# Two attention and gated-MLP layers, one token, float32 cache: larger loads at the ends of passes, one more unit kept on chip, another order of loads

## The chip, the core and the metric

The kernel runs on one core of one Trainium2 chip. The metric is device time in microseconds of one execution, the median of several. The engines are TensorE (PE, with its weight loads as PEld), VectorE (DVE), ScalarE (ACT), GpSimd (POOL) and SyncE (SP); the last one only issues DMAs here. "L364" is line 364 of the kernel before.

## The reference

Two rows x of 448 numbers go twice through an attention block over a cache and a gated MLP. Each (batch, head) pair has 4096 keys and values of 256 numbers, so the caches are 2 x 16 x 4 MiB each and are read in both passes.

```python
B, Sq, D = 2, 1, 448
H, Sk, Dh = 16, 4096, 256          # F = 1792
def _A_ref(x, k_cache, v_cache, wq, wo):
    q = (x @ wq).reshape(B, Sq, H, Dh) ...
    scores = jnp.einsum("bhqd,bhkd->bhqk", q, k_cache) * (Dh ** -0.5)
    p = _softmax(scores, axis=-1)
    o = jnp.einsum("bhqk,bhkd->bhqd", p, v_cache)
    return ... @ wo
def _B_ref(x, W_gate, W_up, W_down):
    gate = gate * (gate > 0);  h = gate * up
    return jnp.einsum("bsf,fd->bsd", h, W_down)
x = x + _A_ref(_layernorm(x), ...)
x = x + _B_ref(_layernorm(x), ...)
x = x + _A_ref(_layernorm(x), ...)
x = x + _B_ref(_layernorm(x), ...)
```

## The kernel before

**Storage.** One SBUF tile, `arena`, has 27 slots ("units") of 128 x 2048 float32, 1 MiB each: six blocks of four slots (0 to 23) and three singles (24 to 26). The keys of one (head, batch) are four units, and so are its values; a head's weights (wq and wo columns) are one unit of 896 KiB; the MLP weights are seven units "in" and four units "out". A "whole" load fills one block with one DMA of 128 x 8192; the other loads fill one slot with 128 x 2048 or 128 x 1792.

**Loads.** `pending` is one list of all loads in the order of issue, and `pump` (L111) issues from its front as long as a place is free: one free slot for a single load, four free slots of one block for a whole one. It is called whenever the program releases a slot. All these DMAs are issued by SP, in order, each waiting on SP until the last reader of its slot is done. They rotate over eight semaphores, so an issue also waits until the load eight places before it has landed. `grouped` (L157) makes whole loads of keys and values except near the ends of a list: `ENDS = 12` keys from the end of a pass are single, and so are the first `SMALL = 25` of pass two.

**Passes.** Pass one runs the 32 steps (0,0), (0,1) ... (15,1), pass two runs them backwards, so its first steps find keys and values that pass one left on chip: `keep` has the 20 first units of pass two, one more unit (the last quarter of the values of step (14,1), `("v", second[2], NC - 1)`) and the weights of head 15. They are not loaded again. That leaves five other slots (two of a block that holds values of (14,1), three singles; the fifth is slot 2) for the MLP weights between the passes. All other keys, values and weights are read again.

**A step u** (`attention`, L280; loop at L502). DVE multiplies keys with the query and reduces (whole and not kept: `score_block`, L355, two multiplications over 16 tiles at L364 and one reduction at L373, while ACT sums eight tiles at L369; unit by unit otherwise: `score`, L378, for a kept unit eight fused instructions at L405, for others L396, L402 and ACT's L398). Then `softmax_max` (L414, L416), `softmax_exp` on ACT (L421, L424), `weigh` on PE (L443: four matmuls per unit), and one step later `out_copy` (ACT, L456), `out_add` (DVE, L459), `out_turn` (PE, L467), `out_keep` (DVE, L476) and `project` (PE, L486). Each engine works in program order. `busy(n)` (L226) is a matmul that nobody reads, put between the last step's quarters of `weigh`.

**The MLP** (`ffn`, L535). `proj` (L545) takes 16 matmuls for the gate (L551; parts 0, 1, 2, 3) and 16 for the up part (3, 4, 5, 6) and releases each "in" unit when it is used up; part 3 holds the last rows of both and is used twice. Then hid is multiplied (L613), transposed (L618, L620), and `block` (L634) computes each of four groups of output columns by 14 matmuls (L641). An ACT copy (L669 in the last layer, L710 in the first) takes each group from PSUM to SBUF. Before, all groups lie side by side in one PSUM region `pd`. In the first layer the four "out" loads, the first keys and two heads' weights of pass two follow the "in" loads in the same queue.

Of the kernel before, what the change touches and what calls it, by code (L numbers as in the profile page):

```python
# [8 lines left out]
F32 = mybir.dt.float32  # L9
AF = mybir.ActivationFunctionType  # L10
# [4 lines left out]
B, D, H, S, DH, F = 2, 448, 16, 4096, 256, 1792  # L15
P = 128
DC = 5
FULL, TAIL = 3, 64
# [3 lines left out]
NC = NT // CT  # L22
# [2 lines left out]

SUMS = 96
SMALL = 25
ENDS = 12
HASTE = 5
CLOSE = 4  # L30
BY_ACT = 3
# [35 lines left out]
def two_layers(  # L67
# [10 lines left out]
    nc = tc.nc  # L78
# [8 lines left out]
    ps_f = ctx.enter_context(tc.tile_pool(name="ps_f", bufs=2, space=PSUM))  # L87
# [7 lines left out]
    pending = []  # L95
# [35 lines left out]
    def get(*key):  # L131
        at = at_of[key]
        return arena[:, at * UNIT : (at + 1) * UNIT]
# [6 lines left out]
    second = first[::-1]  # L140

    def loads(order):
        found = [("h", order[0][0], 0)]
        for u, unit in enumerate(order):
            found.append(("k", unit, 0))
            if u > 0:
                found.append(("v", order[u - 1], 0))
            if u % 2 and u + 1 < len(order):
                found.append(("h", order[u + 1][0], 0))
        return found + [("v", order[-1], 0)]  # L150

    def cut(found):

        for kind, name, c in found:
            yield from ((kind, name, c + k) for k in range(NC if kind in "kv" else 1))

    def grouped(keys, begin, end):  # L157

        keys = list(keys)
        found, i = [], 0  # L160
        while i < len(keys):
            kind, name, c = keys[i]
            whole = kind in "kv" and c == 0 and begin <= i and i + NC <= len(keys) - end
            found.append((keys[i], NC if whole else 1))
            i += found[-1][1]
        return found

    ffn_loads = [("in", "", c) for c in range(7)] + [("out", "", c) for c in range(4)]
    of_first, of_second = list(cut(loads(first))), list(cut(loads(second)))

    keep = {of_second[0], *[key for key in of_second if key[0] != "h"][:KEPT]}
    keep.add(("v", second[2], NC - 1))
    of_second = [key for key in of_second if key not in keep]

    heads = [key for key in of_second if key[0] == "h"][:2]
    of_second = [key for key in of_second if key not in heads]
    of_second[NC - 1 : NC - 1] = heads
    pending += grouped(of_first, 0, ENDS) + [(key, 1) for key in ffn_loads]
    pending += grouped(of_second, SMALL, ENDS) + [(key, 1) for key in ffn_loads]

    row = consts.tile([P, 2 * DH], F32, name="row")
    down = consts.tile([P, D], F32, name="down")
# [35 lines left out]
    po_all = ps_o.tile([P, 2, 2 * DH], F32, name="po")  # L218
# [7 lines left out]
    def busy(n):  # L226


        unread = ps_q.tile([P, n * P], F32, name="pq")
        nc.tensor.matmul(  # L230
            unread[:B], ident[:, :B], ident[:, None, :].to_broadcast([P, n, P]),
            start=True, stop=True,
        )
# [46 lines left out]
    def attention(order, after, q_first=None, begun=None):  # L280
# [6 lines left out]
        n_u = len(order)  # L287
# [147 lines left out]
        def weigh(u, c):  # L435


            vt = get("v", order[u], c)
            if c == 0:
                po_of[u] = po_all[:, u % 2]  # L440
            for t in range(CT // 2):
                n = c * CT + 2 * t
                nc.tensor.matmul(  # L443
                    po_of[u][32 * t : 32 * t + 2, :],
                    p_of[u][:, n : n + 2],
                    vt[:, 2 * t * DH : (2 * t + 2) * DH],
                    start=(c == 0),
                    stop=(c == NC - 1),
                )
            if ("v", order[u], c) not in after:  # L450
                release("v", order[u], c)
            if u == n_u - 1 and c > 0:
                busy(4)

        def out_copy(u):
            nc.scalar.activation(row[:, :DH], po_of[u][:, :DH], AF.Copy, scale=lead[:, 0:1])  # L456
# [78 lines left out]
    def ffn(last):  # L535
# [9 lines left out]
        def proj(parts):  # L545

            p = ps_f.tile([P, D], F32, name="pf")
            for n, (part, c, done) in enumerate(parts):
                w = get("in", "", part)
                for j in range(4):  # L550
                    nc.tensor.matmul(  # L551
                        p[32 * j : 32 * j + 32, :],
                        xs[:, c, :32],
                        w[:, j * D : (j + 1) * D],
                        start=(n == 0),
                        stop=(n == 3),
                    )
                if done:
                    release("in", "", part)
                if part in (4, 5):  # L560
                    between(part)
            return p
# [24 lines left out]

        pg = proj([(0, 0, True), (1, 1, True), (2, 2, True), (3, 3, False)])  # L590
        add_rows(SUMS, lead, stop=last)
        if last:
            y_left = y[:, : FULL * P]
# [37 lines left out]
        stat = [hT[:, m, 32 * j : 32 * j + 32] for j in range(4) for m in range(FULL)]  # L631
        stat += [tails[:, m, :] for m in range(2)]

        def block(pd, c, chunks):  # L634

            width = P if c < FULL else TAIL
            at = slice(c * P, c * P + width)
            w = get("out", "", c)
            for k in chunks:
                g4 = k % 4  # L640
                nc.tensor.matmul(  # L641
                    pd[32 * g4 : 32 * g4 + 32, at], stat[k], w[:, k * width : (k + 1) * width],
                    start=(k < 4), stop=(k >= chunks[-1] - 3),
                )
            return at

        if last:


            square = work.tile([P, B], F32, name="square")  # L650
            nc.vector.tensor_mul(square, rstd, rstd)
            close = work.tile([P, CLOSE, B], F32, name="close")
            for i, st in enumerate(stat[-CLOSE:]):
                nc.vector.tensor_mul(
                    close[:, i, :], square, st.rearrange("p (b r) -> p b r", b=B)[:, :, 0]
                )
            unit = ident[SUMS : SUMS + B, SUMS : SUMS + B]
            y_end = ps_f.tile([P, TAIL], F32, name="pf")[SUMS : SUMS + B]
            nc.tensor.matmul(y_end, unit, y_end_row, start=True, stop=False)
            nc.tensor.matmul(y_left, unit, left, start=True, stop=False)  # L660
            pd = ps_f.tile([P, D], F32, name="pf")

            def to_y(at, stop):
                nc.tensor.matmul(y[:, at], scaled, down[:, at], start=False, stop=stop)

            for c in range(FULL):
                at = block(pd, c, range(14))
                release("out", "", c)
                nc.scalar.activation(down[:, at], pd[:, at], AF.Copy)  # L669
                if c > 0:  # L670
                    to_y(before, False)
                before = at
            at = block(pd, FULL, range(14 - CLOSE))
            nc.scalar.activation(down[:, at], pd[:, at], AF.Copy)
            to_y(before, True)
            nc.vector.tensor_copy(left, y_left)
            nc.sync.dma_start(found[:, : FULL * P], left)
            w = get("out", "", FULL)
            for i in range(CLOSE):
                k = 14 - CLOSE + i  # L680
                w_k = w[:, k * TAIL : (k + 1) * TAIL]
                nc.tensor.matmul(y_end, close[:, i, :], w_k, start=False, stop=False)
            nc.tensor.matmul(y_end, scaled, down[:, at], start=False, stop=True)
            nc.vector.tensor_copy(y_end_row, y_end)
            nc.scalar.dma_start(found[:, FULL * P :], y_end_row)
            return
# [14 lines left out]
                    start=False, stop=(c == FULL + 1),  # L701
                )

        pd = po_all[:, 0, :D]
        sums = work.tile([P, FULL + 1], F32, name="sums4")
        total = work.tile([P, 1], F32, name="sums")
        for c in range(FULL + 1):
            at = block(pd, c, range(14))
            release("out", "", c)
            nc.scalar.activation(down[:, at], pd[:, at], AF.Copy, accum_out=sums[:, c : c + 1])  # L710
            if c > 0:
                ask(c - 1)
            if c == FULL:
                nc.vector.reduce_sum(total, sums, axis=AX.X)
            pt = ps_s.tile([P, B], F32, name="small")
            found_in = [(spans[0][0], c)] if c < FULL else [(p, i.start) for p, i in spans[1:]]
            for p, _ in found_in:
                nc.tensor.matmul(pt[p], down[:, at], scaled, start=True, stop=True)
            for p, i in found_in:
                x_c = xr[p, i]  # L720
                nc.vector.tensor_add(x_c, x_c, pt[p, :, None].to_broadcast(x_c.shape))
# [85 lines left out]
```

## Time and profile before

| | |
|---|---|
| median of 3 runs | 1327.37 us (1326.68 to 1330.33) |
| profiled execution | 1327.61 us, span 1325.7 us |
| busy | PE 581.5, PEld 195.1, DVE 1004.0, ACT 325.1, POOL 106.2 us |
| SP's DMA queue | 562.58 MB, busy 99.5% of 16 engines' span |
| HBM read over the span | 562.56 MB, 424 GB/s |

The span is that of the profiled execution; the 1.9 us between it and its time lie outside of the instructions. In the rows of the timeline the columns are start, duration, engine, line, operation, tiles and count; what stands in brackets is the idle time of the engine just before and what ended it. Pass one ends near 668 us, the first MLP lies between 670 and 693 us, pass two ends near 1303 us and the second MLP runs to the end.

### The profile page before, as it was taken

Reading aid. Unit: us, or ns where it says so; the run is one execution under the profiler, and the core shown is the slowest. Engines: PE = TensorE matmul, PEld = TensorE weight load, DVE = VectorE, ACT = ScalarE, POOL = GpSimd, SP = SyncE. Lnnn points to the kernel's source line nnn. Section 1 sums busy time; section 2 is a strip of 40 time slices with the busy share of each in tenths; the row PEclk is TensorE's granted clock in tenths of the full one; section 3 lists DMA queues with packets and bytes.
Section 4 is the critical chain, followed back from the end, with each engine's and each line's share of the span. In section 5 each row is a group of like instructions: output and inputs, shape, how many; then the busy total and the mean of one; then the engine's idle time right before and its main releaser. Section 6 shows DMA issues by size and latency. Waiting matters only on the chain.

```text
span 1325.7 us, 9957 instructions
## 1 busy us (share of the span) xinstructions
PE 581.5 (44%) x3260; PEld 195.1 (15%) x3260; DVE 1004.0 (76%) x892; ACT 325.1 (25%) x1392; POOL 106.2 (8%) x192
## 2 busy tenths in 40 slices
PE   2434434344343443444584544435345343343438
PEld 2111111111111111111141111111111111111113
DVE  4997877878778787786729888877878778777791
ACT  2221221212212122120026532221212212222131
POOL 0130000000000000000001131000000000000000
PEclk9666566666776766667698677666566665766669
DMA  9999999999999999999999999999999999999997
GB/s 404 429 430 432 429 428 436 426 434 428 430 434 430 432 430 431 431 430 428 417 373 421 428 433 429 434 428 433 429 430 431 430 432 428 434 430 432 429 418 326
DMA packets 30590, 563.20 MB, mean 425 GB/s; under 512 B 3400, under 2 KB 3532, under 8 KB 10316
## 3 DMA queue, kind: packets, MB, share of 16 engines
q1 hardware_dynamic: 30532, 562.58, 99.5%
q8 instruction: 25, 0.41, 0.1%
q14 instruction: 25, 0.20, 0.0%
q10 hardware_dynamic: 8, 0.00, 0.0%
HBM read 562.56 MB, written 0.00 MB: 424 GB/s over the span
## 4 chain that ended last, share of the span: by engine, by line
DMA 68%; DVE 21%; PE 7%; issue 1%; ACT 1%; POOL 1%; DVEq 0%; SPq 0%; POOLq 0%; ACTq 0%
DMA arena<-in_k_cache_dram 50%; DMA arena<-in_w_head_dram 16%; DVE arena L364 10%; DVE scores L373 5%; DVE arena L396 2%; DVE arena L405 2%; DMA arena<-in_v_cache_dram 2%; PE pq L323 1%; PE pf L551 1%; PE acc L486 1%; PE po L443 1%; DVE row L459 1%; DVE scores L402 1%; POOL top L416 1%; ACT arena L398 1%
## 5 line engine op out<-in xcount | busy, mean ns | idle before, releaser
L364 DVE TENSOR_TENSOR arena<-arena 128x4096 f32<-128x4096 f32 x104 | 459.7, 4420 | 210.6 <-DMA arena<-in_k_cache_dram 210.6
L443 PE MATMUL po<-arena,probs 128*2 128x512 f32 x2048 | 316.0, 763 | 106.2 <-DMA arena<-in_v_cache_dram 98.9
L373 DVE TENSOR_REDUCE scores<-arena 128x24 f32<-128x6144 f32 x54 | 352.8, 6534 | 0.0
L467 PE MATMUL small<-ri,row 128*128 128x1 f32 x256 | 62.8, 349 | 460.5 <-DVE row L459 460.5
L369 ACT ACTIVATE arena<-arena 128x256 f32<-128x256 f32 x432 | 173.3, 402 | 290.9 <-DVE arena L364 290.9
L467 PEld LDWEIGHTS small<-ri,row 128*128 128x128 f32 x256 | 57.4, 312 | 520.8 <-DVE row L459 520.8
L421 ACT ACTIVATE nm<-top,nsr 128x1 f32<-128x1 f32 x64 | 18.9, 295 | 372.6 <-POOL top L416 372.6
L443 PEld LDWEIGHTS po<-arena,probs 128*2 128x2 f32 x2048 | 55.7, 98 | 314.3 <-issue 305.3
L486 PE MATMUL acc<-arena,oT 128*2 128x448 f32 x128 | 51.5, 903 | 111.5 <-DVE oT L476 111.5
L416 POOL PARTITION_ALL_REDUCE top<-mx x64 | 50.9, 796 | 611.2 <-DVE mx L414 610.1
L323 PE MATMUL pq<-arena,xs 128*33 128x256 f32 x174 | 75.9, 604 | 42.0 <-DMA arena<-in_w_head_dram 42.0
L369 ACT ACTIVATION_READ_ACCUMULATOR arena<-arena 128x1 f32 x432 | 80.8, 187 | 0.0
L339 POOL PARTITION_BROADCAST arena<-arena x58 | 27.7, 547 | 501.6 <-ACT arena L335 488.7
L335 ACT ACTIVATE arena<-pq 33x256 f32<-33x256 f32 x29 | 10.9, 377 | 203.8 <-PE pq L327 203.8
L459 DVE SCALAR_TENSOR_TENSOR row<-po,lead,row 128x256 f32<-128x256 f32 x64 | 30.7, 480 | 26.5 <-ACT row L456 26.2
L398 ACT ACTIVATE arena<-arena 128x256 f32<-128x256 f32 x97 | 39.0, 404 | 17.6 <-DVE arena L396 17.4
L456 ACT ACTIVATE row<-po,lead 128x256 f32<-128x256 f32 x64 | 29.6, 462 | 51.7 <-PE po L443 51.7
L323 PEld LDWEIGHTS pq<-arena,xs 128*33 128x33 f32 x174 | 25.4, 162 | 111.0 <-issue 96.5
L428 POOL PARTITION_ALL_REDUCE total<-rs x64 | 28.4, 443 | 61.7 <-ACT probs L424 61.7
L405 DVE SCALAR_TENSOR_TENSOR down<-arena,pq 128x256 f32<-128x256 f32 x64 | 26.9, 420 | 8.3 <-DMA arena<-in_k_cache_dram 6.3
L396 DVE TENSOR_TENSOR arena<-arena 128x1024 f32<-128x1024 f32 (+1 forms) x20 | 32.8, 1641 | 0.0
L327 PE MATMUL pq<-arena,xs 128*33 128x128 f32 x116 | 27.6, 384 | 0.0
(144 smaller groups left out, 351.0 us busy)
## 6 DMA issues: line engine op xcount, KB each, us to landing
arena<-in_k_cache_dram SPq DMA_DIRECT2D x56, 4096.0 KB, 45.1
arena<-in_v_cache_dram SPq DMA_DIRECT2D x55, 4096.0 KB, 53.4
arena<-in_w_head_dram SPq DMA_DIRECT2D x31, 896.0 KB, 42.0
arena<-in_v_cache_dram SPq DMA_DIRECT2D x27, 1024.0 KB, 19.8
arena<-in_k_cache_dram SPq DMA_DIRECT2D x20, 1024.0 KB, 16.4
arena<-in_w_in_dram SPq DMA_DIRECT2D x14, 896.0 KB, 19.2
arena<-in_w_out_dram SPq DMA_DIRECT2D x6, 896.0 KB, 9.6
arena<-in_w_out_dram SPq DMA_DIRECT2D x1, 448.0 KB, 8.8
```

The lines of the kernel that those rows point to most:

```text
L323: nc.tensor.matmul(q, xs[:, c, :], w[:, c * DH : (c + 1) * DH], start=(c == 0), stop=False)
L364: nc.vector.tensor_mul(some, some, q_of[u][:, None, :].to_broadcast([P, 2 * CT, DH]))
L369: nc.scalar.activation(kt[:, t, :], kt[:, t, :], AF.Copy, accum_out=s_of[u][:, t : t + 1])
L373: nc.vector.reduce_sum(s_of[u][:, CT:], kt[:, CT:, :], axis=AX.X)
L396: nc.vector.tensor_mul(some, some, q_of[u][:, None, :].to_broadcast([P, whole, DH]))
L398: nc.scalar.activation(kt[:, t, :], kt[:, t, :], AF.Copy, accum_out=found[:, t : t + 1])
L405: nc.vector.scalar_tensor_tensor(junk if kept else kt[:, t, :], kt[:, t, :], 1.0, q_of[u], op0=ALU.mult, op1=ALU.mult, accum_out=found[:, ...
L416: nc.gpsimd.partition_all_reduce(mx_of[u], mx, P, RED.max)
L443: nc.tensor.matmul(po_of[u][32 * t : 32 * t + 2, :], p_of[u][:, n : n + 2], vt[:, 2 * t * DH : (2 * t + 2) * DH], start=(c == 0), stop=(c ...
L459: nc.vector.scalar_tensor_tensor(row[:, :DH], po_of.pop(u)[:, DH:], lead[:, 1:2], row[:, :DH], op0=ALU.mult, op1=ALU.add,)
L467: nc.tensor.matmul(pT_of[u][:, c : c + 1], row[:, c * P : (c + 1) * P], r_of[u], start=True, stop=True,)
L486: nc.tensor.matmul(acc[at : at + B], oT_of[h][:, c, :], wo[:, c * D : (c + 1) * D], start=(n < 3), stop=(n >= n_u - 3),)
```

## The change

There are six edits. (1) The lists are grouped with `ENDS = NC` (4) in pass one and 0 in pass two, so the keys of step (15,1) and the values of (15,0) in pass one, and the keys of (0,0) and the values of (0,1) and (0,0) in pass two, come as whole loads. (2) A 22nd unit of keys and values, `("v", second[2], NC - 2)`, stays on chip. (3) At the start of pass two's list, a key unit and a head's weights alternate. (4) "in" part 3 is loaded and used before part 2 in the gate. (5) The groups of the down projection alternate between the two halves of `po_all` (two PSUM banks). (6) The last step has a further `busy(2)` after its third quarter.

```diff
-ENDS = 12
+ENDS = NC
...
-    ffn_loads = [("in", "", c) for c in range(7)] + [("out", "", c) for c in range(4)]
+    ffn_loads = [("in", "", c) for c in (0, 1, 3, 2, 4, 5, 6)] + [("out", "", c) for c in range(4)]
...
-    keep.add(("v", second[2], NC - 1))
+    keep |= {("v", second[2], c) for c in (NC - 2, NC - 1)}
...
-    of_second[NC - 1 : NC - 1] = heads
+    of_second[1:1], of_second[3:3] = heads[:1], heads[1:]
...
-    pending += grouped(of_second, SMALL, ENDS) + [(key, 1) for key in ffn_loads]
+    pending += grouped(of_second, SMALL, 0) + [(key, 1) for key in ffn_loads]
...
+            if u == n_u - 1 and c == NC - 2:
+                busy(2)
...
-        pg = proj([(0, 0, True), (1, 1, True), (2, 2, True), (3, 3, False)])
+        pg = proj([(0, 0, True), (1, 1, True), (3, 3, False), (2, 2, True)])
...
+        pd = po_all[:, :, :D]
+
-        def block(pd, c, chunks):
+        def block(c, chunks):
...
-                    pd[32 * g4 : 32 * g4 + 32, at], stat[k], w[:, k * width : (k + 1) * width],
+                    pd[32 * g4 : 32 * g4 + 32, c % 2, at],
+                    stat[k],
+                    w[:, k * width : (k + 1) * width],
...
-            pd = ps_f.tile([P, D], F32, name="pf")
...
-                at = block(pd, c, range(14))
+                at = block(c, range(14))
                 release("out", "", c)
-                nc.scalar.activation(down[:, at], pd[:, at], AF.Copy)
+                nc.scalar.activation(down[:, at], pd[:, c % 2, at], AF.Copy)
...
-        pd = po_all[:, 0, :D]
```

On SP, from the last loads of pass one to the first ones of pass two, the difference reads (k_cache and v_cache are keys and values, w_in and w_out the MLP's weights, w_head a head's weights; 128x8192 is a whole load):

```order
-L125 DMA arena<-in_k_cache_dram 128x2048 x4
-L125 DMA arena<-in_v_cache_dram 128x2048 x8
+L125 DMA arena<-in_k_cache_dram 128x8192
+L125 DMA arena<-in_v_cache_dram 128x8192
+L125 DMA arena<-in_v_cache_dram 128x2048 x4
 L125 DMA arena<-in_w_in_dram 128x1792 x7
 L125 DMA arena<-in_w_out_dram 128x1792 x3
 L125 DMA arena<-in_w_out_dram 128x896
-L125 DMA arena<-in_k_cache_dram 128x2048 x3
-L125 DMA arena<-in_w_head_dram 128x1792 x2
 L125 DMA arena<-in_k_cache_dram 128x2048
-L125 DMA arena<-in_v_cache_dram 128x2048 x3
```

Eight single loads became two whole ones; behind the MLP's weights the three keys that came first now alternate with the two heads, and one of the three value units behind them is gone (those rows of the change are not shown). Which slot each load takes follows from the releases: before, "in" 0 to 4 go to slots 25, 0, 1, 2 and 26, and "in" 5 waits for the slot of "in" 0; now slot 2 holds the kept unit, "in" 0, 1, 3 and 2 go to 25, 0, 1 and 26, and "in" 4 waits for the slot of "in" 0.

On DVE, the scores of step 31 of pass one, (15,1), before (scores are kept keys times the query; the row with row and po is `out_add` of step 29):

```order
L405 SCALAR_TENSOR_TENSOR down,scores<-arena,pq 128x256 [waits DMAHW6_49]
L405 SCALAR_TENSOR_TENSOR down,scores<-arena,pq 128x256 [waits DVE_49] x7
L459 SCALAR_TENSOR_TENSOR row<-po,lead,row 128x256 [waits Activation_49]
L405 SCALAR_TENSOR_TENSOR down,scores<-arena,pq 128x256 [waits DMAHW7_49,DVE_49]
L405 SCALAR_TENSOR_TENSOR down,scores<-arena,pq 128x256 [waits DVE_49] x7
L405 SCALAR_TENSOR_TENSOR down,scores<-arena,pq 128x256 [waits DMAHW0_49,DVE_49]
L405 SCALAR_TENSOR_TENSOR down,scores<-arena,pq 128x256 [waits DVE_49] x7
L476 COPY oT<-small 128x2 [waits PE_49]
L433 RECIPROCAL ri<-total 128x1 [waits Pool_49]
L405 SCALAR_TENSOR_TENSOR down,scores<-arena,pq 128x256 [waits DMAHW1_49,DVE_49]
L405 SCALAR_TENSOR_TENSOR down,scores<-arena,pq 128x256 [waits DVE_49] x7
L414 TENSOR_REDUCE mx<-scores 128x1 [waits DVE_49]
```

and now:

```order
L406 SCALAR_TENSOR_TENSOR down,scores<-arena,pq 128x256 [waits DMAHW6_49]
L406 SCALAR_TENSOR_TENSOR down,scores<-arena,pq 128x256 [waits DVE_49] x7
L462 SCALAR_TENSOR_TENSOR row<-po,lead,row 128x256 [waits Activation_49]
L406 SCALAR_TENSOR_TENSOR down,scores<-arena,pq 128x256 [waits DVE_49] x16
L479 COPY oT<-small 128x2 [waits PE_49]
L434 RECIPROCAL ri<-total 128x1 [waits Pool_49]
L406 SCALAR_TENSOR_TENSOR down,scores<-arena,pq 128x256 [waits DVE_49] x8
L415 TENSOR_REDUCE mx<-scores 128x1 [waits DVE_49]
```

The instructions are the same; four waits for a quarter's load each (DMAHW6, 7, 0, 1) became one wait, ahead of the first instruction, for the whole load.

On PE, the end of the first and the start of the later groups of the down projection of the last layer, before (pf is the region `pd`; the row with acc is `to_y`, which reads the ACT copy of the group before):

```order
L641 MATMUL pf<-arena,row 32x128 [waits Activation_49]
L641 MATMUL pf<-arena,row 32x128
L641 MATMUL pf<-arena,row 32x128 [waits DMAHW1_49,Activation_49]
L641 MATMUL pf<-arena,row 32x128 x13
L664 MATMUL acc<-down,scaled 2x128
L641 MATMUL pf<-arena,row 32x128 [waits DMAHW2_49,Activation_49]
```

and now:

```order
L646 MATMUL po<-arena,row 32x128 [waits Activation_49]
L646 MATMUL po<-arena,row 32x128
L646 MATMUL po<-arena,row 32x128 [waits DMAHW1_49,Activation_49]
L646 MATMUL po<-arena,row 32x128 x13
L669 MATMUL acc<-down,scaled 2x128
L646 MATMUL po<-arena,row 32x128 [waits DMAHW2_49,Activation_49]
```

The tile's name changed from pf to po and nothing else: each group's first matmul still waits for ACT, and `to_y` behind it, which needs ACT's copy of the group before, has no wait of its own, so the wait ahead of it covers that copy, as it did.

More of the change, by code (lines that the diff above doesn't have):

```diff
@@ L672, in ffn @@
                 before = at
-            at = block(pd, FULL, range(14 - CLOSE))
-            nc.scalar.activation(down[:, at], pd[:, at], AF.Copy)
+            at = block(FULL, range(14 - CLOSE))
+            nc.scalar.activation(down[:, at], pd[:, FULL % 2, at], AF.Copy)
             to_y(before, True)
@@ L707, in ffn @@
         for c in range(FULL + 1):
-            at = block(pd, c, range(14))
+            at = block(c, range(14))
             release("out", "", c)
-            nc.scalar.activation(down[:, at], pd[:, at], AF.Copy, accum_out=sums[:, c : c + 1])
+            nc.scalar.activation(down[:, at], pd[:, c % 2, at], AF.Copy, accum_out=sums[:, c : c + 1])
             if c > 0:
```

## The prediction

> **What bounds the kernel now.** I read the page's slices first, then the chain, then windows and the timeline of each engine around the two ends of passes.
>
> ```profile
> DMA  9999999999999999999999999999999999999997
> GB/s 404 429 430 432 429 428 436 426 434 428 430 434 430 432 430 431 431 430 428 417 373 421 428 433 429 434 428 433 429 430 431 430 432 428 434 430 432 429 418 326
> DMA 68%; DVE 21%; PE 7%; issue 1%; ACT 1%; POOL 1%; DVEq 0%; SPq 0%; POOLq 0%; ACTq 0%
> 100.00:590.00 490.00, 202.75 (x1031) 62.56 (x1024) 378.69 (x169) 110.83 (x481) 29.14 (x72) 0.65 1.00 431
> 695.00:740.00 45.00, 24.95 (x140) 8.26 (x140) 40.97 (x160) 30.15 (x135) 5.91 (x10) 0.81 1.01 421
> 1270.00:1315.00 45.00, 31.07 (x206) 10.24 (x198) 24.61 (x34) 10.64 (x38) 3.44 (x4) 0.83 1.01 420
> ```
>
> The DMA engines are full except in slice 21 (373 GB/s, about 663 to 696 us) and at the end. The windows (start and end, length, busy time of PE, PEld, DVE, ACT, POOL, granted clock, DMA share, GB/s) say that whole loads run at 431 and single ones at 420 GB/s with the same full share. So the time is bytes over rate, plus the stretches in which the queue has nothing to do, plus what follows the last loads.
>
> **Bytes and rate.** The unit that stays is 1.049 MB: at 420 GB/s **-2.5 us**. Five heads (21.0 MB) go over to whole loads: 49.9 us at 420, 48.7 at 431, together -1.3 us, of which 0.5 in pass one (two heads) and 0.8 in pass two. If nothing else moved, the sum would be -3.8 us. What the ends of the passes do with it is the question.
>
> **The end of pass one.** The rows are DVE's scores of the last two steps, the landing of the last quarter of step 31's keys, and what follows.
>
> ```profile
> 625.51 0.42 DVE L405 SCALAR_TENSOR_TENSOR down<-arena,pq 128x256 f32<-128x256 f32 x1 [6.27 <-DMA arena<-in_k_cache_dram]
> 640.60 0.19 DVE L414 TENSOR_REDUCE mx<-scores 128x1 f32<-128x32 f32 x1
> 640.70 0.41 DVE L405 SCALAR_TENSOR_TENSOR down<-arena,pq 128x256 f32<-128x256 f32 x1
> 655.79 0.19 DVE L414 TENSOR_REDUCE mx<-scores 128x1 f32<-128x32 f32 x1
> L125 SPq DMA_DIRECT2D arena<-in_k_cache_dram x1: 328/328/328, 603.8 to 603.8; - x1
> DMA to landing us min/median/max: 41.2/41.2/41.2
> 659.15 0.47 ACT L456 ACTIVATE row<-po,lead 128x256 f32<-128x256 f32 x1 [1.78 <-PE po L443]
> 660.73 1.90 PE L443 MATMUL po<-arena,probs 128*2 128x512 f32 x16
> 665.42 1.04 PE L443 MATMUL po<-arena,probs 128*2 128x512 f32 x8 [0.24 <-DMA arena<-in_v_cache_dram]
> 671.85 4.46 PE L551 MATMUL pf<-arena,xs 128*32 128x448 f32 x32
> ```
>
> Step 30's keys are a whole load, and DVE sat idle 6.27 us until all of it had landed. Step 31's keys are quarters, and DVE went from step 30 (640.60) into them with no wait, though their last quarter landed only at 603.8 + 41.2 = 645.0. As one whole load they stand at the same place of a full queue, so they land at about 645.0, and DVE, whose first instruction now waits for all, idles 645.0 - 640.7 = **4.3 us**. The maximum moves from 655.8 to 660.1. ACT's `out_copy` of step 30 stands behind step 31's exponential on ACT, but it waited 1.78 us for PE, so by ACT alone it moves 4.3 - 1.8 = 2.5 us. PE moves too: its `project` and step 30's `weigh` stand behind `out_keep`, which is between DVE's scores, so they begin 4.3 us later, and end about 3.3 later, because more of them falls into the full clock. I take 3.3, bounds 2.5 and 4.3. Step 31's `weigh` then starts at 664.0 instead of 660.7. Its quarters have landed by then, so the 0.24 us wait goes, and `busy(2)` adds half of a `busy(4)`, 0.4 us. Without a wait, pass two's last step takes 5.3 us from its first matmul (1295.46, below) to its last (1299.32 + 1.45), so here 5.7: end at 669.7 against 665.42 + 1.04 = 666.5, **+3.2 us**. The MLP's first matmul moves from 671.85 to about 675.1.
>
> **The gap between the passes.**
>
> ```profile
> 665.00:670.00 5.00, 4.01 (x21) 1.06 (x20) 0.64 (x2) 1.07 (x3) 0.00 (x0) 1.00 1.03 424
> 670.00:675.00 5.00, 4.92 (x35) 2.38 (x39) 1.65 (x10) 1.31 (x2) 0.00 (x0) 0.66 0.60 216
> 675.00:680.00 5.00, 5.00 (x40) 1.83 (x32) 0.66 (x4) 0.70 (x2) 0.00 (x0) 1.00 0.91 327
> 680.00:685.00 5.00, 3.90 (x34) 1.78 (x37) 1.18 (x2) 0.76 (x3) 0.00 (x0) 1.00 0.99 400
> 673.62 0.33 SPq L125 DMA_DIRECT2D arena<-in_w_in_dram  x1
> DMA to landing us min/median/max: 4.8/4.8/4.8
> 707.35 0.81 SPq L125 DMA_DIRECT2D arena<-in_k_cache_dram  x2
> ```
>
> Before, five "in" loads fit, and the sixth (673.62) waited for the first gate group to release its slot: 1.8 us after 671.85. The queue lost (420 - 216) x 5 + (420 - 327) x 5 + (420 - 400) x 5 = 1585 KB, that is 3.8 us. Now the 22nd unit holds one of the five slots. The prefetch ends one load (0.918 MB, 2.2 us) and the rate's 0.5 us earlier, and the next load is issued 3.2 us later, at about 676.9. The gap grows by 2.2 + 0.5 + 3.2 = 5.9 us and the bytes shrink by 3.0, so the queue is **2.9 us** behind. The keys that need slots of scored units (707.35, four in all) come with the compute. The sixth load landed 4.8 us after its issue; now the fifth does, so the layer is limited by one more load: 3.2 + 2.2 = 5.4 us later less slack, I take 5. They are issued at about 712.4; with the 1.3 us from issue to first bytes that the gap's end (about 675) shows, they flow at 713.7. What is queued ahead of them, 6.5 MLP loads, two heads and six units, is 14.1 MB, 33.6 us, plus the ramp's loss of 1.3, from 678.2: it would end at 713.1. So 0.6 more (bounds 0 and 1.5): **+3.5 us** in all. Behind that the queue has work, as the 421 GB/s before shows, so this stays to the end. Of it, up to 1.2 us hangs on the clock: the first gate matmuls took 4.46 us at a mean clock of 0.66, and the same 32 in the last layer 3.21.
>
> **The end of pass two.**
>
> ```profile
> L125 SPq DMA_DIRECT2D arena<-in_k_cache_dram x2: 327/380/432, 1233.1 to 1233.5; - x2
> DMA to landing us min/median/max: 42.6/42.6/42.6
> 1259.00 4.43 DVE L364 TENSOR_TENSOR arena<-arena 128x4096 f32<-128x4096 f32 x1 [5.67 <-DMA arena<-in_k_cache_dram]
> 1274.85 0.19 DVE L414 TENSOR_REDUCE mx<-scores 128x1 f32<-128x32 f32 x1
> 1290.57 0.19 DVE L414 TENSOR_REDUCE mx<-scores 128x1 f32<-128x32 f32 x1
> 1293.88 0.47 ACT L456 ACTIVATE row<-po,lead 128x256 f32<-128x256 f32 x1 [1.73 <-PE po L443]
> 1295.46 1.90 PE L443 MATMUL po<-arena,probs 128*2 128x512 f32 x16
> 1299.32 1.45 PE L443 MATMUL po<-arena,probs 128*2 128x512 f32 x5
> 1306.08 3.21 PE L551 MATMUL pf<-arena,xs 128*32 128x448 f32 x32
> 1319.17 0.96 PE L641 MATMUL pf<-arena,row 128*32 128x128 f32 x26 [0.38 <-ACT down L669]
> ```
>
> The same happens with the keys of (0,0). Their third quarter landed at 1233.5 + 42.6 = 1276.1, the fourth one unit (2.5 us) later, 1278.6. DVE was free at 1274.95 and now idles 3.6 us. Then it needs, as a whole step, 1274.85 - 1259.00 = 15.85 us: maximum at 1294.5 against 1290.6, +3.9. Less ACT's 1.73 us of waiting, the last `weigh` starts 2.2 us later; the values of (0,0), now whole, land at about the same time, 1298. With `busy(2)` that is **+2.7 us** to the first matmul of the last MLP (bounds 2.0 and 4.3). The weights land 0.8 us earlier there and nobody waits for them, so that gain is gone.
>
> **PSUM regions.** The later groups of the last projection waited 0.38 us for ACT, three times. The order of the change has the same wait at the same places, so 0, not -1.1. The Trainium skill (PSUM — Partial Sum Buffer, Summary) says to read PSUM from another bank than the one matmuls write; by that the sum would be 1.1 us less. The rows of the order show that PE does not use the freedom here.
>
> **The other edits** cost nothing: "in" part 3 before 2 changes no count, and the heads' earlier places feed a query that is needed ten microseconds later.
>
> **Sum.** 1327.6 (the profiled execution, 0.2 above the median of the runs) + 3.5 + 2.7 = 1333.8: **1334 us**.
>
> **Rivals.**
>
> *Half of it is hidden.* The first matmuls run at the full clock, out_copy alone sets the delay (2.5), and there is no dry stretch after the gap: 5.9 - 0.7 - 1.2 - 3.0 = +1.0 between passes and +2.0 at the end, 1330.6; less, if the MLP's weights land early enough to pull it together. 1328 to 1331. For it: the clock before fell to 0.5 just there. Chance 0.22.
>
> *The ends are not on the path (faster).* If the whole keys are on chip by about 642.5 and 1276.7, that is within the 1.8 us that ACT waited anyway, nothing moves behind DVE, the gap grows only by the slot that the kept unit saves, and bytes and rate decide: 1327.6 - 3.8 = 1323.8. For it: DMA is 68% of the chain, and the last weights land just before they are used. Against it: the 6.27 us that DVE waited for a whole load one step earlier. Chance 0.1. The Trainium skill (DMA: Bandwidth & Descriptors, Bandwidth, Measured) goes further: a fixed 2.0 us per DMA, so larger ones pay; fifteen fewer loads would give 30 us less, 1294, an estimate by that page. The windows speak against it: 420 to 431 GB/s at a full share, loads overlap. Chance 0.01.
>
> *The refill starves.* With one slot fewer every load between 677 and 720 waits for a release, and each dry spell costs the 1.3 us from issue to bytes: three more of them, about 1338 to 1341. Chance 0.07.
>
> **How the numbers follow.** The forecast has 0.6, with its own range from 1331 (all low bounds: +1.8 and +2.0) to 1337.5 (+5.5 and +4.3). 0.3% of the median, about what a measurement tells from no change, is 4 us: slower is above 1331.4, faster below 1323.4. Slower: 0.6 less 0.04 at its low end, plus 0.07: 0.63. Faster: half of the fast rival, 0.06. The same: 0.31. The range 1326 to 1338 leaves out most of the fast rival and the starving one.
>
> **What would show it.** Right: DVE idle of about 4 us at its first L406 of step 31 and 3.6 us before the last L365 pair; the fifth "in" load issued near 677; a deeper low than 216 GB/s there. Wrong: no idle at these two places, or the MLP starting before 673, or the ACT waits in the last projection gone.

## The result, and the profile after

| | before | after |
|---|---|---|
| median | 1327.43 us (6 runs) | 1337.23 us (6 runs, 1335.76 to 1340.69) |
| profiled execution | 1327.61 us, span 1325.7 | 1338.10 us, span 1336.3 |
| HBM read | 562.56 MB | 561.52 MB |

The ratio is 1.0071, with a 95% interval from 1.0054 to 1.0088: slower by 9.4 us. The median is inside the range, 3.2 us above the forecast. The page of the changed kernel has these slices and this chain:

```profile
DMA  9999999999999999999979999999999999999996
GB/s 400 434 429 433 428 429 436 426 431 430 431 431 431 431 430 433 426 434 431 417 277 392 432 424 437 430 427 433 432 428 432 431 429 431 429 431 434 426 427 273
DMA 66%; DVE 21%; PE 8%; issue 2%; POOL 1%; ACT 1%; DVEq 0%; SPq 0%; POOLq 0%; ACTq 0%
```

Two places differ: slices 21 and 22 (277 and 392 GB/s against 373 and 421), and the last one (273 against 326), where more time is left behind the last load. All else runs at the same rate. Windows of the stretch between the passes, the last two columns DMA share and GB/s, before:

```profile
655.00:695.00 40.00, 35.33 (x315) 15.38 (x306) 8.68 (x43) 8.34 (x29) 0.74 (x2) 0.93 0.95 381
695.00:720.00 25.00, 10.98 (x66) 4.91 (x70) 24.37 (x97) 17.66 (x78) 3.39 (x6) 0.84 1.01 421
```

and after:

```profile
655.00:695.00 40.00, 33.23 (x248) 12.65 (x249) 9.55 (x46) 5.75 (x16) 0.74 (x2) 0.87 0.75 301
670.00:675.00 5.00, 4.17 (x25) 1.41 (x17) 0.68 (x3) 1.60 (x4) 0.00 (x0) 1.00 0.11 47
675.00:680.00 5.00, 5.00 (x40) 2.18 (x43) 1.61 (x10) 0.79 (x1) 0.00 (x0) 0.66 0.16 41
695.00:720.00 25.00, 15.49 (x134) 7.74 (x133) 20.62 (x87) 15.03 (x67) 1.71 (x4) 0.86 1.00 377
715.00:720.00 5.00, 3.31 (x24) 0.48 (x16) 5.00 (x20) 3.42 (x16) 0.00 (x0) 0.85 0.97 331
```

Up to 695 us the queue loses (381 - 301) x 40 / 420 = 7.6 us more than before, from 695 to 720 another (421 - 377) x 25 / 420 = 2.6. Less 3.0 us for the unit that is not loaded and the better rate, the queue should be 7.2 us behind. The timeline at the end of pass one shows where this begins (start, duration, engine, line, operation, tiles; in brackets the idle time and what ended it):

```profile
644.58 0.42 DVE L406 SCALAR_TENSOR_TENSOR down<-arena,pq 128x256 f32<-128x256 f32 x1 [4.06 <-DMA arena<-in_k_cache_dram]
659.68 0.19 DVE L415 TENSOR_REDUCE mx<-scores 128x1 f32<-128x32 f32 x1
656.98 6.31 PE L444 MATMUL po<-arena,probs 128*2 128x512 f32 x30
663.36 0.47 ACT L459 ACTIVATE row<-po,lead 128x256 f32<-128x256 f32 x1 [2.11 <-PE po L444]
676.31 4.50 PE L554 MATMUL pf<-arena,xs 128*32 128x448 f32 x32
678.08 0.33 SPq L125 DMA_DIRECT2D arena<-in_w_in_dram  x1
```

VectorE waits 4.06 us for the whole keys, the maximum comes 3.9 us later, ScalarE's copy, which waits for TensorE, 4.2, the MLP's first matmul 4.5, and the fifth "in" load is issued 4.5 us later than the sixth one was before. The end of pass two:

```profile
1266.54 4.43 DVE L365 TENSOR_TENSOR arena<-arena 128x4096 f32<-128x4096 f32 x1 [5.70 <-DMA arena<-in_k_cache_dram]
1285.87 4.42 DVE L365 TENSOR_TENSOR arena<-arena 128x4096 f32<-128x4096 f32 x1 [3.29 <-DMA arena<-in_k_cache_dram]
1305.44 1.90 PE L444 MATMUL po<-arena,probs 128*2 128x512 f32 x16 [0.62 <-DMA arena<-in_v_cache_dram]
1316.71 3.21 PE L554 MATMUL pf<-arena,xs 128*32 128x448 f32 x32
1329.80 0.96 PE L646 MATMUL po<-arena,row 128*32 128x128 f32 x26 [0.38 <-ACT down L674]
```

The keys of (0,1) are there 7.5 us later (1266.54 against 1259.00): that is what the middle cost in these two executions. The last MLP begins 10.6 us later (1316.71 against 1306.08), so the end of pass two adds 3.1. From there on nothing changed; the wait for ScalarE in the last projection is still 0.38 us. 7.5 + 3.1 = 10.6, the difference of the two spans.

### The profile page after: what moved, and what is told of

It is laid out like the page before. It is cut to its first block, busy times and chain, and to the rows that moved or that the text cites. A ratio compares the mean times of both kernels' runs of the same rounds, so it can differ in the third digit from the quotient of the medians.

```text
span 1336.3 us, 9919 instructions
## 1 busy us (share of the span) xinstructions
PE 589.4 (44%) x3264; PEld 196.2 (15%) x3264; DVE 1004.6 (75%) x887; ACT 323.3 (24%) x1384; POOL 100.5 (8%) x192
## 3 DMA queue, kind: packets, MB, share of 16 engines
HBM read 561.52 MB, written 0.00 MB: 420 GB/s over the span
## 4 chain that ended last, share of the span: by engine, by line
DMA 66%; DVE 21%; PE 8%; issue 2%; POOL 1%; ACT 1%; DVEq 0%; SPq 0%; POOLq 0%; ACTq 0%
DMA arena<-in_k_cache_dram 44%; DMA arena<-in_w_head_dram 19%; DVE arena L365 10%; DVE scores L374 5%; DMA arena<-in_v_cache_dram 3%; DVE arena L397 2%; PE pq L324 2%; DVE arena L406 2%; POOL top L417 1%; PE po L444 1%; PE acc L489 1%; PE pf L554 1%; DVE down L406 1%; DVE row L462 1%; DMA arena<-in_w_in_dram 1%
## 5 line engine op out<-in xcount | busy, mean ns | idle before, releaser
L365 DVE TENSOR_TENSOR arena<-arena 128x4096 f32<-128x4096 f32 x106 | 468.5, 4420 | 213.7 <-DMA arena<-in_k_cache_dram 213.7
L444 PE MATMUL po<-arena,probs 128*2 128x512 f32 x2048 | 321.1, 773 | 107.2 <-DMA arena<-in_v_cache_dram 101.1
L374 DVE TENSOR_REDUCE scores<-arena 128x24 f32<-128x6144 f32 x55 | 359.3, 6533 | 0.0
L417 POOL PARTITION_ALL_REDUCE top<-mx x64 | 48.8, 762 | 626.9 <-DVE mx L415 625.8
L429 POOL PARTITION_ALL_REDUCE total<-rs x64 | 24.8, 387 | 61.7 <-ACT probs L425 61.7
L425 ACT ACTIVATE probs<-scores,nm,sr 128x32 f32<-128x32 f32 x64 | 26.4, 413 | 2.1
```

Of the source, the lines that this page charges most:

```text
L365: nc.vector.tensor_mul(some, some, q_of[u][:, None, :].to_broadcast([P, 2 * CT, DH]))
L374: nc.vector.reduce_sum(s_of[u][:, CT:], kt[:, CT:, :], axis=AX.X)
L417: nc.gpsimd.partition_all_reduce(mx_of[u], mx, P, RED.max)
L444: nc.tensor.matmul(po_of[u][32 * t : 32 * t + 2, :], p_of[u][:, n : n + 2], vt[:, 2 * t * DH : (2 * t + 2) * DH], start=(c == 0), stop=(c ...
```

## The experiments

Each ratio is to runs of the kernel before on the same chip, over five rounds (three where said), with its 95% interval. 1.0010 is 1.3 us.

**One end at a time.** In the kernel before, pass one alone and pass two alone:

```diff
-    pending += grouped(of_first, 0, ENDS) + [(key, 1) for key in ffn_loads]
+    pending += grouped(of_first, 0, NC) + [(key, 1) for key in ffn_loads]
```

> The kernel before, with whole loads at the end of pass one only (15,1) keys, (15,0) values. Theory: the wait for the whole load of the keys of (15,1) delays TensorE's weigh(30), (31) and the MLP's first matmul by 4.3 to 4.5 us, so the sixth MLP load is issued that much later and everything behind it: 1327.4 + 4.4 - 0.5 (rate) + 0.5 (gap) = 1331.8, from 1331 to 1333. First matmul of the first MLP 4 to 4.5 us later. Rival A (size as first predicted, 3.2): 1330.6. Rival B (the end of pass one is not on the path; the queue has enough ahead): 1326.9.

```diff
-    pending += grouped(of_second, SMALL, ENDS) + [(key, 1) for key in ffn_loads]
+    pending += grouped(of_second, SMALL, 0) + [(key, 1) for key in ffn_loads]
```

> The kernel before, with whole loads at the end of pass two only (keys of (0,0), values of (0,1) and (0,0)). Theory: VectorE waits about 3.6 us ahead of its last pair of multiplications, ScalarE's slack of 1.7 us takes some, the last MLP starts 2.3 to 2.7 us later: 1329.7 to 1330.1. Rival (the weights at the end are what counts, and they land 0.8 us earlier): 1326.6.

Measured: 1.0024 (1.0014 to 1.0034) and 1.0028 (1.0017 to 1.0039), that is 3.2 and 3.7 us. Both ends are on the path. The first came out at rival A's size, though its interval reaches into the theory's range (from 1.0027); the second came out above the theory. In the second, two waits stand behind one another:

```profile
1277.67 4.42 DVE L364 TENSOR_TENSOR arena<-arena 128x4096 f32<-128x4096 f32 x1 [3.29 <-DMA arena<-in_k_cache_dram]
1297.21 3.31 PE L443 MATMUL po<-arena,probs 128*2 128x512 f32 x16 [0.59 <-DMA arena<-in_v_cache_dram]
```

VectorE waits for the whole keys, and TensorE, late by that, waits another 0.59 us for the whole values. The 16 matmuls behind that wait then took 3.31 us at a mean granted clock of 0.58, where they took 1.90 us at the full clock before and in the changed kernel: 1.4 us of this execution that the theory did not have.

**The 22nd unit alone** in the kernel before, and the changed kernel without it:

```diff
-    keep.add(("v", second[2], NC - 1))
+    keep |= {("v", second[2], c) for c in (NC - 2, NC - 1)}
```

> The kernel before, with only the 22nd unit kept on chip. Theory: 2.5 us less to load, 2.2 us more gap since one load fewer fits ahead of it, and behind the gap loads go out one by one as slots are released, up to 2.5 us lost between 695 and 720 us: 1327.4 - 0.3 + 0 to 2.5 = 1327.1 to 1329.6, likeliest 1328.5. Rival (bytes alone decide): 1324.9.

```diff
-    keep |= {("v", second[2], c) for c in (NC - 2, NC - 1)}
+    keep.add(("v", second[2], NC - 1))
```

> The changed kernel without its 22nd unit (21 kept as before), all else of the change in place. Theory: the two ends alone cost 4.4 and 2.7 to 3.1, so 1327.4 + 7.3 = 1334.7 (1334 to 1335.5), and the thin stretch from 700 to 720 us (407, 379, 354, 331 GB/s in the changed kernel) is back near 420. Rival (the unit costs nothing, the ends cost all of it): 1337.2. Rival (the unit saves its 2.5 us): 1339.7.

Measured: 1.0032 (1.0020 to 1.0044) for the unit alone, more than the theory; 1.0060 (1.0047 to 1.0072) for the change without it, at the theory's upper end. So the unit costs 4.2 us in the kernel before, and in the changed kernel what it costs (1.0071 against 1.0060) is within the intervals. The unit alone had a hole of another kind. Windows, and SP's issues in the same stretch:

```profile
685.00:690.00 5.00, 3.31 (x47) 1.64 (x46) 1.18 (x2) 1.28 (x5) 0.00 (x0) 1.00 1.01 424
690.00:695.00 5.00, 5.00 (x96) 3.70 (x96) 0.68 (x4) 1.05 (x6) 0.00 (x0) 1.00 0.43 130
695.00:720.00 25.00, 14.16 (x69) 5.92 (x68) 18.86 (x84) 13.64 (x60) 1.69 (x4) 0.73 0.96 368
```
```profile
686.29 0.33 SPq L125 DMA_DIRECT2D arena<-in_w_out_dram  x1
693.11 6.51 SPq L125 DMA_DIRECT2D arena<-in_k_cache_dram  x3
699.66 0.91 SPq L125 DMA_DIRECT2D arena<-in_w_head_dram  x2
```

For 6.8 us nothing is issued. The front of the list is a key unit, which `take` (L42) puts only into slots of blocks; the first slots that come free are singles, which the heads behind it could use. (Before, the five slots between the passes are 0, 1 and 2 of a block and two singles, 25 and 26; the count of three singles ahead of the prediction is wrong. With the unit, slot 2 is taken, so only two of the free ones can hold a key: the third key waits for a scored unit, and the heads behind it go out at 699.66 only.) The late heads explain much of the thin stretch behind the hole. TensorE's query of head 14 waits for its weights, ScalarE's copy of that query waits for TensorE, and behind the copy stands ScalarE's share of the last scores of (15,1), for which VectorE waits:

```profile
707.15 2.74 PE L323 MATMUL pq<-arena,xs 128*33 128x256 f32 x6 [5.85 <-DMA arena<-in_w_head_dram]
710.78 0.38 ACT L335 ACTIVATE arena<-pq 33x256 f32<-33x256 f32 x1 [6.75 <-PE pq L327]
712.39 0.19 DVE L414 TENSOR_REDUCE mx<-scores 128x1 f32<-128x32 f32 x1 [5.08 <-ACT arena L398]
```

So the slots of scored units come free later, and between 704.48 and 712.39 us no load is issued.

**The unit with turns** (edits 2 and 3 in the kernel before):

```diff
-    keep.add(("v", second[2], NC - 1))
+    keep |= {("v", second[2], c) for c in (NC - 2, NC - 1)}
...
-    of_second[NC - 1 : NC - 1] = heads
+    of_second[1:1], of_second[3:3] = heads[:1], heads[1:]
```

> The kernel before with the 22nd unit and with key units and heads by turns (edits 2 and 3). The kernel with the unit alone ran dry from 690 to 695 us (130 GB/s): the front of the list was a key unit, heads behind it could have used the single slots that were free. Theory: the turns fill that hole, 2 to 3.4 us less than the unit alone (1.0032): ratio 1.0010 to 1.0017, 690 to 695 us near 400 GB/s. Rival (the hole only moves, since the slots in flight are too few either way): the same ratio as the unit alone, 1.003.

Measured: 1.0012 (1.0003 to 1.0022), as the theory has it, but not by its way:

```profile
685.00:690.00 5.00, 4.25 (x84) 3.13 (x86) 0.94 (x3) 1.17 (x6) 0.00 (x0) 1.00 0.70 287
690.00:695.00 5.00, 4.93 (x68) 3.13 (x60) 1.71 (x9) 1.50 (x8) 0.00 (x0) 1.00 0.67 236
695.00:720.00 25.00, 9.95 (x58) 4.59 (x58) 24.36 (x98) 17.55 (x78) 3.40 (x6) 0.79 1.01 422
```

The hole is still there (a key is still at the front), so the theory's way fell, and its number came out by another. The stretch behind the hole is full, where the unit alone had 368 GB/s: (422 - 368) x 25 / 420 = 3.2 us. The heads now go out at 691.35 and 692.60, and the query no longer waits:

```profile
698.80 1.48 PE L323 MATMUL pq<-arena,xs 128*33 128x256 f32 x6
```

So by these rows the turns gain the earlier query and not the hole.

**Edits 3 to 6 alone** (the changed kernel with edits 1 and 2 undone), and the same without busy(2):

```diff
-    keep |= {("v", second[2], c) for c in (NC - 2, NC - 1)}
+    keep.add(("v", second[2], NC - 1))
...
-ENDS = NC
+ENDS = 12
...
-    pending += grouped(of_second, SMALL, 0) + [(key, 1) for key in ffn_loads]
+    pending += grouped(of_second, SMALL, ENDS) + [(key, 1) for key in ffn_loads]
```

> Edits 3 to 6 alone (turns of keys and heads, order of the MLP's third part, two PSUM regions, busy(2)); single loads at the ends and 21 units as before. Theory: busy(2) costs 0.4 us at each of the two ends, the rest nothing: 0.4 to 0.8 us, ratio 1.0003 to 1.0006. Rival (the turns also fill holes with 21 units, or the regions free TensorE): 0.999 to 0.9995. Rival (the sum of the parts tried so far leaves the rest to these edits): 1.001 or more.

> Edits 3 to 5 alone (turns, order of the third part, two PSUM regions), without busy(2). With busy(2) they came to 1.0013 (1.0003 to 1.0024), more than the 0.4 us at each end that were reckoned for it. Theory: busy(2) makes up all of it, 1.0000 to 1.0004 without it. Rival: the turns or the order of the parts cost 1 to 2 us between the passes, and it stays at 1.0010 to 1.0015.

Measured: 1.0013 (1.0003 to 1.0024) and, with these two lines out as well, 1.0010 (1.0001 to 1.0019).

```diff
-            if u == n_u - 1 and c == NC - 2:
-                busy(2)
```

That is the rival's number, though the interval still takes in the theory's upper end (1.0004); the two ratios differ by less than the noise, so what busy(2) costs is not shown. SP and the windows without busy(2) show the mirror image of the unit alone:

```profile
682.35 0.33 SPq L125 DMA_DIRECT2D arena<-in_k_cache_dram  x1
689.46 0.33 SPq L125 DMA_DIRECT2D arena<-in_w_head_dram  x1
```
```profile
690.00:695.00 5.00, 3.72 (x47) 2.37 (x46) 2.92 (x17) 2.31 (x11) 0.00 (x0) 1.00 0.90 279
```

Now a head stands at the front and waits for a single slot, and the keys behind it could have gone out. (420 - 279) x 5 / 420 = 1.7 us; over 655 to 695 us, where part of the gap is won back, 369 GB/s against 381 before make 1.1 us. In the changed kernel, with 22 units and the third part loaded before the second, the slots come free in turns as the list needs them, and this hole is not there: its loads of 693.04, 694.89, 696.82 and 698.24 are key, head, key, head.

**Which whole loads hurt.** The changed kernel with the last keys of each pass in quarters (three rounds), then with the last values too:

```diff
         found, i = [], 0
+        end_keys = [key for key in keys if key[0] == "k"][-1][1]
...
-            whole = kind in "kv" and c == 0 and begin <= i and i + NC <= len(keys) - end
+            whole = (kind, name) != ("k", end_keys) and kind in "kv" and c == 0 and begin <= i and i + NC <= len(keys) - end
```

> The changed kernel with the last keys of each pass (those of (15,1) and of (0,0)) in quarters again, the values at the ends still whole. Theory: the whole keys alone cost the ends of the passes; the first MLP starts near 672, VectorE does not wait ahead of the last step, 5 to 6.5 us less than the changed kernel: ratio to before 1.002 to 1.0035. Rival (the whole values do it as well, since weigh of the last step waits for all of them): about the changed kernel, 1.006 to 1.007.

```diff
         found, i = [], 0
+        last = [[key for key in keys if key[0] == kind][-1][:2] for kind in "kv"]
...
-            whole = kind in "kv" and c == 0 and begin <= i and i + NC <= len(keys) - end
+            whole = (kind, name) not in last and kind in "kv" and c == 0 and begin <= i and i + NC <= len(keys) - end
```

> The changed kernel with the last keys and the last values of each pass in quarters: (15,1) and (0,0); whole remain the values of (15,0) and (0,1). Theory: each last load costs the end of pass two about 3 us by itself, the keys through VectorE, the values through TensorE's weigh, and side by side no more than one of them; with both in quarters these 3 us go, and in pass one 1 to 2 us stay for the whole values of (15,0), which delay weigh of step 30. Unit with turns 1.0012, plus that: 1.002 to 1.003. Rival (the whole values of the last step but one delay as much as the last ones): 1.005 to 1.007. Rival (all the cost was in the last loads): 1.0012 or less.

Measured: 1.0073 (1.0057 to 1.0088), so the theory fell and the time is the rival's; and 1.0042 (1.0029 to 1.0055), between theory and rival. TensorE in pass one and pass two of the first, and in pass one of the second:

```profile
655.20 6.09 PE L445 MATMUL po<-arena,probs 128*2 128x512 f32 x32 [1.69 <-DMA arena<-in_v_cache_dram]
1300.97 2.68 PE L445 MATMUL po<-arena,probs 128*2 128x512 f32 x16 [2.50 <-DMA arena<-in_v_cache_dram]
```
```profile
655.73 6.51 PE L445 MATMUL po<-arena,probs 128*2 128x512 f32 x32 [2.06 <-DMA arena<-in_v_cache_dram]
```

With the keys in quarters VectorE is on time again, and TensorE waits for the whole values instead: in pass one weigh(30) for those of (15,0), in pass two weigh(31) for those of (0,0). From the keys of (0,1) to the first matmul of the last MLP it is 47.1 us before, 50.2 in the changed kernel, 52.1 with the last keys in quarters and 48.8 with the last values too: at the end of pass two the whole values are enough by themselves. In pass one they delay the first MLP as well, but in this execution to 674.23, 2.4 us later than before, where the changed kernel has 4.5. That the whole keys alone would be enough is not shown: no run has them without whole values.

**PSUM in two tiles**, in the last layer of the kernel before:

```diff
-            pd = ps_f.tile([P, D], F32, name="pf")
+            pds = [ps_f.tile([P, D], F32, name="pf"), po_all[:, 0, :D]]
...
+                pd = pds[c % 2]
                 at = block(pd, c, range(14))
...
+            pd = pds[FULL % 2]
             at = block(pd, FULL, range(14 - CLOSE))
```

> The kernel before, with the down groups of the last layer in two PSUM tiles by turns instead of one (the change has two regions of one tile). Here the order has no wait for ScalarE ahead of a group; to_y waits, one group later. Theory: three waits of 0.36 to 0.38 us go, 1.1 us less, ratio 0.9992. Rival (the last weights land just in time, so the wait for ScalarE becomes one for them, or TensorE pays the same in to_y): 1.0000.

Measured: 0.9989 (0.9980 to 0.9998), the one version below the kernel before. The three waits for ScalarE are gone, one for weights came in their place:

```profile
1320.57 0.96 PE L641 MATMUL pf<-arena,row 128*32 128x128 f32 x26 [0.59 <-DMA arena<-in_w_out_dram]
```

**20 units** in the kernel before (the last quarter of the values of (14,1) is loaded again), and **more busy matmuls** in it (three rounds):

```diff
-    keep.add(("v", second[2], NC - 1))
```

> The kernel before with 20 units kept instead of 21: 1.05 MB more to load (+2.5 us), one more slot for the MLP's weights between the passes. Theory: the sixth load goes out ahead of the pass's end, most of the gap's loss of 3.8 us goes (2.2 to 3 us), no more since nothing starves there: ratio 0.9997 to 1.0002. Rival (a slot is worth as much on this side as on the other, 4 us of gap and refill): 0.9988. Rival (the gap is set by the first gate matmuls, not by slots): 1.0019.

```diff
-                busy(2)
+                busy(4)
+                busy(4)
...
-        busy(1)
+        busy(4)
+        busy(4)
```

> The kernel before with more matmuls that nobody reads at the end of the last step and ahead of the first gate matmul (two busy(4) in place of busy(2), two in place of busy(1)). Theory: the half clock in the first gate group (4.46 us where the last layer takes 3.21) comes from idle time just before; it goes, all later loads come 1.2 us earlier: ratio 0.999. Rival (the clock follows something else, or the added matmuls delay the start by what they save): 1.0000 to 1.0008.

Measured: 1.0020 (1.0010 to 1.0029) and 1.0014 (1.0005 to 1.0023); both theories fell. With 20 units the stretch from 655 to 695 us moved 393 GB/s against 381:

```profile
655.00:695.00 40.00, 33.75 (x317) 15.23 (x311) 9.67 (x47) 9.29 (x34) 0.74 (x2) 0.99 0.98 393
670.00:675.00 5.00, 4.88 (x47) 2.33 (x48) 1.64 (x10) 1.15 (x1) 0.00 (x0) 1.00 0.95 376
675.00:680.00 5.00, 5.00 (x37) 1.91 (x33) 0.66 (x4) 0.70 (x2) 0.00 (x0) 1.00 1.01 415
```

That is 1.1 us won for 2.5 us of bytes. The number is the last rival's, nearly, but its reason is not: the gap did shrink with the slot, from 216 and 327 GB/s to 376 and 415, which is 3.0 us and what the theory had. The next 15 us gave 1.9 of it back (377, 318 and 393 GB/s against 400, 420 and 427): from 678 to 684.77 us nothing is issued, since a key stands at the front and the first free slots are singles, as with the unit alone. With more busy matmuls the clock was full in the first gate group (28 of its 32 matmuls took 3.14 us), but the group began 1.8 us later (673.69).

## Why the prediction was right, and where its sizes were off

- **Right: whole loads at the ends delay both MLPs.** VectorE's idle times were 4.06 and 3.29 us (forecast 4.3 and 3.6), and each end alone made the kernel slower. But every cost came out at its forecast or above, and 1337.2 lies just below the upper bound of the forecast's own range, 1337.5.
- **End of pass one, forecast +3.2, measured +4.5.** The step "end about 3.3 later, because more of them falls into the full clock" failed. weigh(30) took no less than before in this execution, so the upper bound of 4.3 was the value. Its row before, and the window of the changed kernel with the granted clock third from the end:

```profile
653.09 5.99 PE L443 MATMUL po<-arena,probs 128*2 128x512 f32 x30
```
```profile
655.00:660.00 5.00, 3.94 (x20) 1.31 (x24) 4.52 (x24) 0.00 (x0) 0.00 (x0) 0.50 1.01 420
```

It ended at 659.1 before and at 663.3 now (656.98 + 6.31), 4.2 us later; up to 660 us it got half the clock. Part of this is chance: with the same whole loads, weigh(30) took 5.48 us in the profile without the unit and 5.36 in that of pass one alone, and the first matmul of the MLP came 3.7 and 3.0 us later, around the forecast.
- **The gap and the stretch behind it, forecast +5.9 and +0.6, measured +7.6 and +2.6.** 1.3 of the first 1.7 is the later first matmul. The second is the step "Behind that the queue has work, as the 421 GB/s before shows": the keys of 707.35 were issued at 714.53, 7.2 us later and not 5, and while the loads from 703 us on wait for scored units, the queue behind them runs thin. This is the starving rival, given 0.07, beside the forecast and not in its place. It takes the unit: without it the changed kernel moved 419 GB/s there:

```profile
695.00:720.00 25.00, 10.73 (x63) 4.34 (x61) 23.93 (x100) 16.85 (x74) 3.13 (x6) 0.83 1.01 419
```

  The unit by itself is not enough for it: the unit with turns, its ends in quarters, moved 422 there and lost 3.8 us earlier, from 685 to 695 us. The 368 GB/s of the unit alone had another cause, the late query. What the unit costs beside the whole loads is within the intervals, as said above, so the 2.6 us is a reading of windows.

- **End of pass two, forecast +2.7, measured +3.1.** Right in size, with one cause of two: the whole values, which were given no cost, held TensorE as long when the keys came in quarters. (The terms as the prediction gives them, 2.2 and 0.4, make 2.6.)
- **PSUM regions, forecast 0: right.** The waits of 0.38 us stayed, and the two tiles show what they are worth. The Trainium skill (PSUM — Partial Sum Buffer, Summary) advises reading from another bank than the one being written. The two-tile run agrees, with 0.9989; the two regions of one tile are two banks as well and gain nothing, since the order still waits.
- **The other edits, forecast 0: not so.** With 21 units edits 3 to 5 cost 0.0010 (1.0001 to 1.0019). Beside the 22nd unit the turns gained 0.0020: the step "the heads' earlier places feed a query that is needed ten microseconds later" failed there, since the query waited 5.85 us without them. Edits 4 to 6 beside the unit were not tried alone.
- **Against the rivals:** "the ends are not on the path" and "bytes alone decide" fell with each of the runs on ends and unit. The estimate of 1294 fell too: sixteen loads fewer came with 9.4 us more. (The Trainium skill gives those 2.0 us per DMA under Anatomy of one DMA, for DMAs issued from GpSimd; here SP issues.) Parts add up: 0.0024 + 0.0028 for the ends, 0.0013 for edits 3 to 6, 0.0065 in all against 0.0060 measured together.

What stays open: whether the whole keys alone, with all values in quarters, cost pass one as much as both; and how much of the 2.7 us that the turns gained beside the unit is the earlier query. The gate group took 4.56 us in the profile of the unit alone, first of these rows, and 3.37 in that with turns, so chance in the clock may hold part of it.

```profile
672.33 4.56 PE L551 MATMUL pf<-arena,xs 128*32 128x448 f32 x32
```
```profile
671.68 3.37 PE L551 MATMUL pf<-arena,xs 128*32 128x448 f32 x32
```

## What to carry to other kernels

At the end of a pass nothing hides a load's last bytes, so what the last consumers read should come in pieces, and every consumer counts: with the keys in quarters, the values still held the end of pass two. A unit kept on chip saves its bytes but takes a slot from the loads in flight; the price shows in the stretch where the queue lives on released slots, not in the bytes. A small load behind a blocked one can hold up more than the queue: with the unit alone the weights of a head came late, with them the query, and with it the slots. One ordered list over two kinds of slots stalls when the front needs the kind that is not free, and which order is right changes with the number of slots.

## What was not expected of the hardware

The same 32 gate matmuls took from 3.21 to 5.93 us, by the granted clock. The two extremes are the last layer of the kernel before, shown with the prediction, and the first layer with whole loads at the end of pass one alone, where the granted clock was 0.50 from 675 to 680 us; the last layer of edits 3 to 5 without busy(2), the second row, comes next:

```profile
674.87 5.93 PE L551 MATMUL pf<-arena,xs 128*32 128x448 f32 x32
1307.17 5.85 PE L552 MATMUL pf<-arena,xs 128*32 128x448 f32 x32
```

In the first layer of the unit with turns, with the same matmuls ahead of the group as before, they took 3.37 us (above), before 4.46.

The Trainium skill (TensorE: Matmul & The Clock Gate, Part 1) says that the window over which activity is judged runs freely and does not start with the kernel. That fits this difference between runs; no run here shows the window itself. Up to 2.7 us in one group of matmuls may be one reason why single executions of one kernel lie up to 8 us apart (edits 3 to 6: 1327.1 to 1335.0). Rows that differ by 1 or 2 us between two profiles can be chance, and differences of that size are read here from intervals over many runs.
